# Moving the last segment's memory reads from the projections into the attention, on GpSimd's queue

## The chip, the cores and the metric

The kernel runs on one core of one Trainium2 chip. A core has TensorE (PE, matrix products; PEld is its weight loads), VectorE (DVE), ScalarE (ACT) and GpSimd (POOL), each with an instruction queue of its own that runs in order, and SyncE (SP), which issues most of the transfers. Transfers can also be issued from the queues of GpSimd and ScalarE. The metric is the device time of one execution in microseconds (us).

## The reference

Two attention layers on sequences of 2048 rows with 576 columns, 32 heads of 18, side by side in the output. A is softmax attention whose heads share one key and one value. B is cut into four segments of 512 rows and adds a memory that is filled segment by segment:

```python
phi = lambda t: jnp.where(t > 0, t + 1.0, jnp.exp(t))
for s in range(N):
    qs, ks, vs = q[:, :, s], k[:, :, s], v[:, :, s]
    logits = jnp.einsum("bhqd,bhkd->bhqk", qs, ks) * scale + mask
    p = _softmax(logits, axis=-1)
    a_dot = jnp.einsum("bhqk,bhkd->bhqd", p, vs)
    pq = phi(qs)
    num = jnp.einsum("bhld,bhde->bhle", pq, M)
    den = jnp.einsum("bhld,bhd->bhl", pq, z)[..., None] + 1e-6
    o = g * (num / den) + (1.0 - g) * a_dot
    outs.append(o)
    pk = phi(ks)
    M = M + jnp.einsum("bhld,bhle->bhde", pk, vs)
    z = z + jnp.einsum("bhld->bhd", pk)
```

To *ask the memory* is to compute `num` and `den` of a segment from its features `phi(q)`. The first segment's memory is empty, so three segments ask: s = 1, 2 and 3 (the last).

## The kernel before

**Stage 1, projections (to about 277 us).** A's chunks are projected, then B's segments s = 0 to 3. Every operand is a high and a low part, so one projection of 126 columns is 14 matmuls (L261). For each segment PE computes keys, values (14 matmuls for each quarter of rows and half of the heads, L513) and queries; ACT and DVE split the results in two parts and form features (L408, L414, L416); SP and ACT store them to DRAM. B's weights come in 15 parts on GpSimd's queue into buffers `wr`, two in each of two pools (L242), and are split by ACT (L251) and POOL (L252); the last three parts (12 to 14) are loaded within the key projections of s = 0, each after the split of an earlier part. For s = 3 the four last query projections are interleaved with this segment's asks: numerators `ask` (L444), evictions with the gate's factor (L451), denominators `total` (L592); beside them the bounds for the softmax (`bound`, L588), whose sum DVE reduces to `fm` (L613) and turns into a shift (L136).

**Stage 2, attention (277 to about 1365 us).** The order is written out by hand in 416 *turns* of three items. PE computes the scores E of an item (A: L945, B: L953), ACT its exponentials (L963); the second item of a turn is first copied by DVE from E to W (L960), and single halves are exponentials on DVE alone (L919 to L926, `BY_DVE`). Two turns later PE multiplies P with the values into O (L993). In B POOL clears the masked part of P in between (`affine_select`, L968). A block of A is 11 turns, a block of B two: A has turns 0 to 10, B 11 to 18, A 19 to 29, B 30 to 37, A 38 to 48, B 49 to 52, and so on. PE gets one piece of *fill* a turn: in turns 0 to 18 by the table `LATER` pieces of the four last values' sums that stage 1 left over (`late_value`, pairs of quarter and number of matmuls); from turn 20 (`ASK`) the asks of the segments in `LATE_ASK`, s = 1 and 2, as long as they last and only in turns of A; then the output projection (L796).

An ask in the attention (L852) comes in pieces of four matmuls, eight in the trace's records, for half of the columns; two pieces make one answer, which DVE writes over the features (L857). The features of a segment are loaded by `load_qf` from `qfB` into a tile `xh`, of which there are two, so that a third segment's features take the place of the first that were asked. The answers go from that tile to `numB` and `denB` by `store`, two turns after the ask. All these transfers are SP's. They are read back much later, when a segment's heads are weighed (`place` holds that back until enough segments are asked).

Of the kernel before, what the change touches and what calls it, by code (L numbers as in the profile page):

```python
# [8 lines left out]
F32 = mybir.dt.float32  # L9
# [13 lines left out]
C = 512  # L23
# [55 lines left out]
def attention_pair_kernel(ctx, tc, a_xT, a_w, a_wo, b_xT, b_w, b_wo, b_beta, ident_d, hmask_d, bmask_d, cmask_d, sel_d, zmask_d, selx_d, sely_d, out):  # L79
# [82 lines left out]
    with ExitStack() as ph:  # L162
# [256 lines left out]
        for s in range(NSEG):  # L419
# [19 lines left out]

            def ask(t, hold=lambda ins: ins):  # L440
                R = RT[t]
                pn = ps.tile([128, C], F32, name="mm", bufs=1)
                hold(
                    nc.tensor.matmul(  # L444
                        pn[:R], Mst[:R, t].rearrange("p h d -> p (h d)")[:, :R], fs[t][:R], start=True, stop=True
                    )
                )

                def answer():
                    nm = p2.tile([128, C], F32, name="nm", bufs=2)  # L450
                    hold(nc.scalar.activation(nm[:R], pn[:R], AF.Copy, scale=gt[:R, t : t + 1]))  # L451
                    nc.sync.dma_start(numB[s][126 * t : 126 * t + R], nm[:R])

                return answer


            for t in range(5):
# [18 lines left out]
                if not last or t == 4:  # L476
                    f = phi(pj[:126], 126, "kf" if t < 4 else "qf", 2 if t < 4 else 5, hold, e[0])
                    if t == 4:
                        fs[4] = f
# [23 lines left out]

            def value_sums(xh, xl, i, hf, pj, m0=0, m1=14):
                ops = []
                tk = slice(128 * i, 128 * i + 128)
                n = 288 if hf else 306
                for k in range(5):
                    hi, lo = (wv[:, k, 0], wv[:, k, 1]) if hf else (wBh[:, k, 1134:1440], wBl[:, k, 1134:1440])
                    ops += [(xh[:, k, tk], hi)] + ([(xl[:, k, tk], hi)] if k < 4 else []) + [(xh[:, k, tk], lo)]  # L510
                for m, (x, w) in enumerate(ops):
                    if m0 <= m < m1:
                        nc.tensor.matmul(pj[:, :n], x, w, start=m == 0, stop=m == len(ops) - 1)  # L513

            def values(i, hf):
                pj = ps.tile([128, C], F32, name="pj" if hf else "nd", bufs=4 if hf else 2)
                value_sums(xh, xl, i, hf, pj)
# [50 lines left out]
            for t in range(4) if not last else []:  # L568
# [8 lines left out]
                if s:  # L577
                    fs[t] = phi(pj[:126], 126, "qf", 5, e=e[0])
                    nc.sync.dma_start(qfB[s][:126, t], fs[t][:126])
# [9 lines left out]

            def total(pd, t):  # L590
                R, rows = RT[t], slice(32 * (t % 4), 32 * (t % 4) + 32)
                pin(nc.tensor.matmul(pd[rows], zst[:R, t], fs[t][:R], start=t < 4, stop=t > 0))  # L592

            for t in range(4) if last else []:
                pj = ps.tile([128, C], F32, name="pj", bufs=4)
                proj(pj[:126], wBh, wBl, xh, xl, 126 * t, 126, pin)
                answer = ask(t - 1 if t else 4, pin)
                if t < 2:
                    (fifth_bound if t else last_key)(pin)
                if t == 3:  # L600
                    pu, pd = (ps.tile([128, C], F32, name="nd", bufs=2) for _ in range(2))
                    for i in (0, 1, 2, 4):
                        total(pd, i)
                e = negative(pj[:126], 126, pin)
                magnitude(t, pj, pin)
                fs[t] = phi(pj[:126], 126, "qf", 5, pin, e)
                answer()
                if t == 3:
                    for i in range(5):
                        bound(pu, i, pin)  # L610
                    answer = ask(3, pin)
                    total(pd, 3)
                    pin(nc.vector.tensor_reduce(fm[:, 1 + s : 2 + s], pu, axis=AX.X, op=ALU.max))  # L613
                qp = split2(pt, pj[:126], 126, pin)
                store_parts(qp, 0, 126, qB[s], 7 * t, 7)
                if t == 3:
                    answer()
                    dn = p2.tile([128, C], F32, name="ph_e", bufs=2)
            if not last:
# [6 lines left out]
            if last:  # L626
                nc.vector.tensor_scalar(dn, pd, 1e-6, None, op0=ALU.add)
                nc.sync.dma_start(denB[s], dn)
                def late_value(i, m0, m1, pj, v, xh=xh, xl=xl, value_sums=value_sums):
# [197 lines left out]
    def load_qf(s):  # L827
        qfs[s] = px.tile([128, 5, C], F32, name="xh")
        nc.sync.dma_start(qfs[s][:126, :4], qfB[s][:126, :4])
        nc.sync.dma_start(qfs[s][: RT[4], 4], qfB[s][: RT[4], 4])  # L830

    def ask_memory():
# [5 lines left out]
        for s in LATE_ASK:  # L838
            qf = qfs[s]
            for t in (-1, 0, 1, 2, 3, 4):  # L840
# [22 lines left out]
                def store(k, s=s, t=t, qf=qf, dn=dn):  # L863
                    if t < 0:
                        nc.sync.dma_start(denB[s], dn)
                    elif t == 4:
                        nc.sync.dma_start(numB[s][126 * t :], qf[: RT[4], 4])
                        nc.sync.dma_start(denB[s][7:11], dn[103:107])
                        asked[0] = s
                    elif t == 3:  # L870
                        nc.sync.dma_start(numB[s][: 126 * 4].rearrange("(t r) c -> r t c", r=126), qf[:126, :4])

# [140 lines left out]
    def by_dve(c, hg):  # L1013

        return [x for n, x in enumerate(BY_DVE) if n < 2 or (c, hg) in third]

# [49 lines left out]
    def finish(k, ab, c, hg):  # L1066
# [64 lines left out]
    with tc.manual_schedule(engines={ENG.PE, ENG.Activation, ENG.DVE}):  # L1131
# [75 lines left out]

        for k in range(len(turns) + 2):
            now[0] = k
            exps = [scores(its[n], pr, i == 1) for i, (n, pr) in enumerate(turns[k])] if k < len(turns) else []  # L1210
            for i in (0, 2, 1) if len(exps) == 3 else range(len(exps)):
                exps[i]()
            if k in FLAG:
                loose_flag(k)
            if k < len(LATER) and LATER[k]:
                i, m = LATER[k]
                m0, pj = begun_value.pop(i) if i in begun_value else (0, psO.tile([128, C], F32, name="O" if i == 3 else "F"))
                if m0 + m < 14:
                    begun_value[i] = m0 + m, pj
                late_value(i, m0, m0 + m, pj, (pa.tile([128, D], F32, name="osb", bufs=2) if i > 1 else pa.tile([128, C], F32, name="oe", bufs=4))[:, :304] if m0 + m == 14 else None)  # L1220
            if k > len(turns):
                halve_heads(first, 0)
            if memory is None:
# [355 lines left out]
```

## Time and profile before

| | us |
|---|---|
| median of 3 runs (lowest to highest) | 1393.98 (1393.3 to 1396.08) |
| the profiled execution | 1394.57 |
| its span in the trace | 1392.9 |
| busy: ACT, DVE, POOL | 1205.8, 1032.6, 260.5 |

All times of rows in this document count from the start of the span of the profiled execution; granted clock 0.999. A row of the chain or of a timeline has the start, the duration and what ran, `x14` being fourteen instructions in one; a row of the waits has the waiting instruction, what it waited for, the sum of the time, how often and the longest. Matmul records overlap, since matmuls are pipelined: the distance between two starts is what one costs, not its record. Behind a transfer in the list of issues stand its KB and the median us from issue to landing.

### The profile page before, as it was taken

To read this page: it belongs to the slowest core of one execution; us is meant where nothing else is said; L and a number is where in the kernel's file an instruction comes from. 1 tells how busy PE (TensorE), PEld (TensorE's weight loads), DVE (VectorE), ACT (ScalarE), POOL (GpSimd) and SP (SyncE) were. 2 spreads that over 40 slices of the span, in tenths; PEclk is the share of its full clock that TensorE was granted. 3 is DMA by queue.
4 is the path that set the end of the run, shared out by engine and by line. 5 is a ranking of instruction groups with operands and counts; after the bars stand their busy time and mean duration, and the time that the engine had idled before them with its cause. 6 is when DMAs were issued, how large, how long until landed. Compare 5 with 4: busy or idle time off the path is not lost.

```text
span 1392.9 us, 41210 instructions
## 1 busy us (share of the span) xinstructions
PE 1379.1 (99%) x17455; PEld 835.6 (60%) x17455; DVE 1032.6 (74%) x1509; ACT 1205.8 (87%) x1497; POOL 260.5 (19%) x388
## 2 busy tenths in 40 slices
PE   9999999999999999999999999999999999999998
PEld 6778888755554555555555555555555555555558
DVE  6565463388787887777888877876878778887884
ACT  4543453599999999999999999999999999999992
POOL 2462120012313211312110022113010220001002
PEclk9999999999999999999999999999999999999999
DMA  9876556575564545332322442232103321120023
GB/s 285 261 230 185 180 198 204 188 208 181 153 182 158 147 145 162 101 113 77 105 67 71 141 152 63 85 120 79 52 35 100 104 76 42 31 71 21 18 64 132
DMA packets 88638, 173.67 MB, mean 125 GB/s; under 512 B 12308, under 2 KB 20109, under 8 KB 88018
## 3 DMA queue, kind: packets, MB, share of 16 engines
q1 hardware_dynamic: 81614, 158.91, 36.6%
q0 software_dynamic: 2368, 7.13, 1.8%
q10 hardware_dynamic: 4464, 4.92, 1.1%
q8 instruction: 139, 2.28, 0.7%
q14 instruction: 53, 0.43, 0.1%
HBM read 99.65 MB, written 70.67 MB: 122 GB/s over the span
## 4 chain that ended last, share of the span: by engine, by line
PE 88%; DVE 4%; ACT 3%; DMA 2%; issue 1%; POOL 1%; SPq 0%; DVEq 0%; POOLq 0%; ACTq 0%
PE O L993 33%; PE E L945 20%; PE F L796 11%; PE pj L261 11%; PE E L953 3%; ACT P L963 3%; PE nd L513 2%; DVE W L960 2%; PE pj L513 2%; PE E L1280 2%; PE pj L293 1%; PE F L852 1%; PE F L513 1%; DMA wr<-b_w 1%; DMA vseg<-vB 0%
## 5 line engine op out<-in xcount | busy, mean ns | idle before, releaser
L963 ACT ACTIVATE P<-E 128x1024 f32<-128x1024 f32 (+1 forms) x800 | 783.4, 1066 | 2.0 <-PE E L945 1.6
L960 DVE COPY W<-E 128x1024 f32<-128x1024 f32 (+2 forms) x416 | 453.1, 1089 | 142.2 <-PE E L945 84.1
L993 PE MATMUL O<-P,VA 128*32 128x256 f32 x7504 | 506.8, 379 | 0.0
L963 ACT ACTIVATE P<-W 128x1024 f32<-128x1024 f32 (+1 forms) x330 | 366.8, 1112 | 6.8 <-DVE W L960 6.3
L993 PEld LDWEIGHTS O<-P,VA 128*32 128x32 f32 x7504 | 258.8, 110 | 137.7 <-issue 4.7
L945 PE MATMUL E<-xl,kstA 56*128 56x512 f32 x1920 | 317.3, 430 | 2.1 <-ACT P L963 1.8
L945 PEld LDWEIGHTS E<-xl,kstA 56*128 56x128 f32 x1920 | 155.0, 184 | 159.1 <-issue 94.7
L968 POOL TENSOR_SCALAR_AFFINE_SELECT P<-P 128x256 f32<-128x256 f32 (+1 forms) x192 | 94.6, 493 | 393.4 <-ACT P L963 384.1
L780 POOL TENSOR_TENSOR xh<-xh,rb 126x512 f32<-126x512 f32 (+1 forms) x55 | 70.7, 1308 | 428.7 <-DVE PD L926 185.1
L796 PE MATMUL F<-woB,xh 126*32 126x192 f32 (+1 forms) x1920 | 126.6, 338 | 0.0
L993 PE MATMUL O<-PD,VA 128*32 128x256 f32 x688 | 88.9, 379 | 0.0
L796 PEld LDWEIGHTS F<-woB,xh 126*32 126x32 f32 (+1 forms) x1920 | 38.6, 108 | 74.8 <-issue 69.6
L993 PE MATMUL O<-P,vseg 128*32 128x256 f32 (+2 forms) x1536 | 81.4, 344 | 0.3
L127 DVE TENSOR_TENSOR qp<-pj,qp 126x512 fp32r<-126x512 f32 (+1 forms) x54 | 36.9, 686 | 54.4 <-ACT ph_e L408 32.8
L1002 DVE COPY oe<-O 128x512 f32<-128x512 f32 x64 | 44.2, 691 | 42.6 <-PE O L993 40.8
L261 PE MATMUL pj<-xh,wBh 128*126 128x512 f32 x180 | 72.5, 403 | 0.0
L919 DVE TENSOR_SCALAR PD<-E 128x512 uint32<-128x512 f32 x86 | 59.2, 688 | 16.5 <-PE E L945 14.9
L261 PE MATMUL pj<-xh,wBl 128*126 128x512 f32 x180 | 71.0, 394 | 0.0
L125 ACT CAST qp<-pj 126x512 fp32r<-126x512 f32 (+1 forms) x54 | 31.5, 584 | 42.6 <-PE pj L261 32.6
L993 PEld LDWEIGHTS O<-P,vseg 128*32 128x32 f32 x1536 | 49.1, 110 | 25.3 <-issue 1.8
L796 PE MATMUL F<-woA,xh 126*32 126x192 f32 (+1 forms) x960 | 63.9, 338 | 0.0
L924 DVE SCALAR_TENSOR_TENSOR PD<-PD,n 128x512 f32<-128x512 f32 x86 | 59.5, 692 | 3.0
(238 smaller groups left out, 1570.1 us busy)
## 6 DMA issues: line engine op xcount, KB each, us to landing
stB<-kB SPq DMA_DIRECT2D x96, 144.0 KB
stB<-qB SPq DMA_DIRECT2D x32, 288.0 KB
xl<-qA SPq DMA_DIRECT2D x30, 288.0 KB
oA<-oe SPq DMA_DIRECT2D x32, 256.0 KB
oB<-oe SPq DMA_DIRECT2D x32, 256.0 KB
qA<-qp SPq DMA_DIRECT2D x16, 504.0 KB
kB<-qp SPq DMA_DIRECT2D x16, 504.0 KB
qB<-qp SPq DMA_DIRECT2D x16, 504.0 KB
```

Of the source, the lines that this page charges most:

```text
L261: hold(nc.tensor.matmul(dst, w[:, c0 : c0 + M], x, start=i == 0, stop=i == len(ops) - 1))
L513: nc.tensor.matmul(pj[:, :n], x, w, start=m == 0, stop=m == len(ops) - 1)
L780: ins = tc.keep_in_program_order(nc.gpsimd.tensor_tensor(dst, a, b, op=op))
L796: nc.tensor.matmul(dst[32 * j : 32 * j + 32], parts[ab, c][: RT[t], t, r0 : r0 + 32], wo[ab][: RT[t], t, c0 : c0 + n], start=start, stop=stop,
L919: v.tensor_scalar(y, e, EXP_A, EXP_B, op0=ALU.mult, op1=ALU.add)
L924: lambda: stt(p, p, POLY[1], u, op0=ALU.add, op1=ALU.mult),
L945: nc.tensor.matmul(e[:, j], kstA[rows, 128 * kt : 128 * kt + 128], st[rows, h, :], start=True, stop=True)
L960: gate.append(nc.vector.tensor_copy(src[:, hs, :n], e[:, hs, :n]))
L963: nc.scalar.activation(p[:, hs, :n], src[:, hs, :n], AF.Exp, scale=SCALE)
L968: nc.gpsimd.affine_select(diag, diag, pattern=[[0, 2], [0, m], [1, 128]], base=0, channel_multiplier=-1, compare_op=ALU.is_ge, fill=0.0)
L993: nc.tensor.matmul(o[32 * j : 32 * j + 32, q0 : q0 + n], v, p[:, j % 2, p0 : p0 + n], start=m == hf == 0, stop=last and hf == 1,)
L1002: nc.vector.tensor_copy(osb, o)
```

## The change

The parts that belong together:

- Segment 3 is asked in the attention too. `ask`, `answer`, `total`, the evictions and the stores leave stage 1; its features go to `qfB[3]` instead. `ask_memory` now yields in every turn from 20 on, those of B too, so that 36 pieces take the turns 20 to 55, as 24 took before.
- The transfers of asks (`load_qf`, `store`) are issued from GpSimd's queue. The features of segment 3 are loaded at turn 32 or later, when the first asked segment is stored.
- The values' sum of quarter 2 (`values(2, 1)`) is back in stage 1; `LATER` has three others, done by turn 7.
- The weight parts 12 to 14 have buffers of their own and are loaded as soon as these exist.
- The first block has no half on DVE, and turn 0 no copy W; feature buffers go from five to three; `place` waits for one segment more.

```diff
-LATE_ASK, ASK = (1, 2), 20
-LATER = [(2, 14), (3, 14), (0, 3), None, (0, 3), (0, 4), None, (0, 4), None, None, (1, 3), None, (1, 3), None, (1, 2), (1, 2), (1, 2), None, (1, 2)]
+LATE_ASK, ASK = (1, 2, 3), 20
+LATER = [(3, 14), (0, 14), (1, 3), None, (1, 3), (1, 4), None, (1, 4)]
...
-            wrs[i] = (p1 if i % 2 and i < 10 else pt).tile([128, 648], F32, name="wr", bufs=2)[:, :n]
+            if i < 12:
+                wrs[i] = (p1 if i % 2 and i < 10 else pt).tile([128, 648], F32, name="wr", bufs=2)[:, :n]
+            else:
+                wrs[i] = p2.tile([128, 504], F32, name="wr2", bufs=3)
...
         p2 = ph.enter_context(tc.tile_pool(name="p2", bufs=1))
+        for i in (12, 13, 14):
+            load_wpart(i)
...
-                    if t < 3:
-                        load_wpart(12 + t)
-            if s and not last:
+            if s:
                 nc.sync.dma_start(qfB[s][: RT[4], 4], fs[4][: RT[4]])
...
                 proj(pj[:126], wBh, wBl, xh, xl, 126 * t, 126, pin)
-                answer = ask(t - 1 if t else 4, pin)
                 if t < 2:
                     (fifth_bound if t else last_key)(pin)
-                if t == 3:
-                    pu, pd = (ps.tile([128, C], F32, name="nd", bufs=2) for _ in range(2))
-                    for i in (0, 1, 2, 4):
-                        total(pd, i)
                 e = negative(pj[:126], 126, pin)
                 magnitude(t, pj, pin)
-                fs[t] = phi(pj[:126], 126, "qf", 5, pin, e)
-                answer()
+                qp = split2(pt, pj[:126], 126, pin)
+                store_parts(qp, 0, 126, qB[s], 7 * t, 7)
+                f = phi(pj[:126], 126, "qf", 3, pin, e)
+                nc.sync.dma_start(qfB[s][:126, t], f[:126])
                 if t == 3:
+                    values(2, 1, "mm", 1)
+                    pu = ps.tile([128, C], F32, name="nd", bufs=2)
                     for i in range(5):
                         bound(pu, i, pin)
-                    answer = ask(3, pin)
-                    total(pd, 3)
                     pin(nc.vector.tensor_reduce(fm[:, 1 + s : 2 + s], pu, axis=AX.X, op=ALU.max))
...
-        nc.sync.dma_start(qfs[s][:126, :4], qfB[s][:126, :4])
-        nc.sync.dma_start(qfs[s][: RT[4], 4], qfB[s][: RT[4], 4])
+        nc.gpsimd.dma_start(qfs[s][:126, :4], qfB[s][:126, :4])
+        nc.gpsimd.dma_start(qfs[s][: RT[4], 4], qfB[s][: RT[4], 4])
...
-                        nc.sync.dma_start(denB[s], dn)
+                        nc.gpsimd.dma_start(denB[s], dn)
...
-        return [x for n, x in enumerate(BY_DVE) if n < 2 or (c, hg) in third]
+        return [x for n, x in enumerate(BY_DVE) if (n or c or hg) and (n < 2 or (c, hg) in third)]
...
-            return (ab, c) in parts or len(parts) - filled[0] // FILL < 2 and asked[0] >= min(2, len(parts) + 1)
+            return (ab, c) in parts or len(parts) - filled[0] // FILL < 2 and asked[0] >= min(3, len(parts) + 2)
...
         at(ASK + 4, 0, lambda: True, lambda k: load_qf(2))
+        at(ASK + 12, 0, lambda: asked[0] >= 1, lambda k: load_qf(3))
...
-            elif k >= ASK and all(its[n][0] == "A" for n, pr in turns[k]) and next(memory, None) is None:
+            elif k >= ASK and next(memory, None) is None:
```

How the change moves instructions shows in the order of the engines' programs. POOL's rows at the start of B's first segment, before (`wr` are raw weight parts, `wBl` their low halves, `Mbd` the memory, `bands` the mask's bands):

```order
L242 DMA wr<-b_w 128x504
L395 MEMSET Mbd 128x285
L396 MEMSET mx 128x285
...
L402 MEMSET mz 128x790
L501 MEMSET vch 128x128
L252 TENSOR_TENSOR wBl<-wr,wBh 128x504
L242 DMA wr<-b_w 128x504
L252 TENSOR_TENSOR wBl<-wr,wBh 128x504
L242 DMA wr<-b_w 128x504
L252 TENSOR_TENSOR wBl<-wr,wBh 128x504
L242 DMA wr<-b_w 64x504 x2
```

And of the change:

```order
L245 DMA wr<-b_w 128x504
L245 DMA wr_856<-b_w 128x504
L245 DMA wr_858<-b_w 128x504
L245 DMA wr_860<-b_w 64x504 x2
L400 MEMSET Mbd 128x285
```

The last four transfers, for three parts, moved ahead of the clearing and of every split that stood between them.

PE's rows from the end of the last projection to the second score, before (`nd<-qf,mz` are totals, `mm<-qf,mz` an ask, `nd<-aq,kbB` bounds, `E<-st_126,kstA` scores):

```order
L261 MATMUL pj<-xh,wBl 126x512
L444 MATMUL mm<-qf,mz 126x512
L592 MATMUL nd<-qf,mz 32x512 x4
L588 LDWEIGHTS kbB
L588 MATMUL nd<-aq,kbB 32x512
...
L444 MATMUL mm<-qf,mz 126x512
L592 MATMUL nd<-qf,mz 32x512
L945 MATMUL E<-st_126,kstA 128x512 x6
```

Of the change (`mm<-woB,xh` are the values' matmuls, 14 in all):

```order
L264 MATMUL pj<-xh,wBl 126x512
L499 MATMUL mm<-woB,xh 128x288
L499 MATMUL mm<-woB,xl 128x288
...
L574 LDWEIGHTS kbB
L574 MATMUL nd<-aq,kbB 32x512
L918 MATMUL E<-st_127,kstA 128x512 x6
L499 MATMUL O<-woB,xh 128x288
```

Asks and totals are gone, and a values' sum stands ahead of the bounds; behind the first scores comes a late value in the bank O, where before it was F.

PE's rows in a turn of B from turn 30 on, before (scores `E<-stB`, products `O<-P,vseg`):

```order
L953 MATMUL E<-stB 128x512 x4
L953 MATMUL E<-stB 128x384 x2
L993 MATMUL O<-P,vseg 32x256 x8
L993 MATMUL O<-P,vseg 32x192 x4
L953 MATMUL E<-stB 128x384 x2
```

Of the change:

```order
L926 MATMUL E<-stB 128x512 x4
L926 MATMUL E<-stB 128x384 x2
L825 MATMUL F<-xh,woA 32x256 x4
L966 MATMUL O<-P,vseg 32x256 x8
L966 MATMUL O<-P,vseg 32x192 x4
L926 MATMUL E<-stB 128x384 x2
```

The four matmuls of a piece of an ask, which the trace records as eight, stand between the scores and the products of every B turn from 30 to 37 and from 49 to 52.

POOL's rows in the turns 30 to 33; before, these are masks alone (`P<-P`) at this place. Of the change:

```order
L838 DMA denB_111<-rb 128x512
L844 DMA numB_107<-xh 126x4x512
L941 AFFINE_SELECT P<-P 128x2x128 x4
L941 AFFINE_SELECT P<-P 128x4x128
L840 DMA numB_107<-xh 72x512
L941 AFFINE_SELECT P<-P 128x4x128
L841 DMA denB_111<-rb 4x512
L941 AFFINE_SELECT P<-P 128x2x128
L802 DMA xh<-qfB_116 126x2048
L941 AFFINE_SELECT P<-P 128x2x128 x3
L941 AFFINE_SELECT P<-P 128x4x128
L803 DMA xh<-qfB_116 72x512
```

The stores of segment 1's answers (1008 KB, then 144 KB, `numB`) and the load of segment 3's features into the same tile (`xh<-qfB`) now stand between the masks, in the queue that both share.

More of the change, by code (lines that the diff above doesn't have):

```diff
@@ L438, in magnitude @@
                 hold(nc.scalar.activation(aqs[t][:R], pj[:R], AF.Abs))
[L440 to L454, printed above, removed]
             for t in range(5):
@@ L512, in value_sums, with values @@
                     if m0 <= m < m1:
[L513 to L517, printed above, removed]
+                        hold(nc.tensor.matmul(pj[:, :n], x, w, start=m == 0, stop=m == len(ops) - 1))
+            def values(i, hf, nm=None, bufs=None):
+                pj = ps.tile([128, C], F32, name=nm or ("pj" if hf else "nd"), bufs=bufs or (4 if hf else 2))
+                value_sums(xh, xl, i, hf, pj, hold=pin if last else lambda ins: ins)
                 hs = slice(16 * hf, 16 * hf + 16)
@@ L577, in attention_pair_kernel @@
                 if s:
-                    fs[t] = phi(pj[:126], 126, "qf", 5, e=e[0])
+                    fs[t] = phi(pj[:126], 126, "qf", 3, e=e[0])
                     nc.sync.dma_start(qfB[s][:126, t], fs[t][:126])
@@ L588, in bound @@
                 hold(nc.tensor.matmul(pu[rows], kbB[:R, t], aqs[t][:R], start=t < 4, stop=t > 0))
-            def total(pd, t):
-                R, rows = RT[t], slice(32 * (t % 4), 32 * (t % 4) + 32)
-                pin(nc.tensor.matmul(pd[rows], zst[:R, t], fs[t][:R], start=t < 4, stop=t > 0))
             for t in range(4) if last else []:
@@ L864, in store @@
                     if t < 0:
-                        nc.sync.dma_start(denB[s], dn)
+                        nc.gpsimd.dma_start(denB[s], dn)
                     elif t == 4:
-                        nc.sync.dma_start(numB[s][126 * t :], qf[: RT[4], 4])
-                        nc.sync.dma_start(denB[s][7:11], dn[103:107])
+                        nc.gpsimd.dma_start(numB[s][126 * t :], qf[: RT[4], 4])
+                        nc.gpsimd.dma_start(denB[s][7:11], dn[103:107])
                         asked[0] = s
                     elif t == 3:
-                        nc.sync.dma_start(numB[s][: 126 * 4].rearrange("(t r) c -> r t c", r=126), qf[:126, :4])
+                        nc.gpsimd.dma_start(numB[s][: 126 * 4].rearrange("(t r) c -> r t c", r=126), qf[:126, :4])
                 at(now[0] + 2, 0, lambda: True, store)
@@ L1206, in halve_heads, with late_values @@
             mixed(x[:88, 1], hi[:88, 1], raws[key], some[:88, 1:2])
[L1208 to L1214, printed above, removed]
+        def late_values(k):
             if k < len(LATER) and LATER[k]:
@@ L1220, in attention_pair_kernel @@
                 late_value(i, m0, m0 + m, pj, (pa.tile([128, D], F32, name="osb", bufs=2) if i > 1 else pa.tile([128, C], F32, name="oe", bufs=4))[:, :304] if m0 + m == 14 else None)
+        for k in range(len(turns) + 2):
+            now[0] = k
+            if k == 0:
+                psE.tile([128, 2, 512], F32, name="E")
+            exps = []
+            for i, (n, pr) in enumerate(turns[k]) if k < len(turns) else []:
+                exps.append(scores(its[n], pr, i == 1 and k > 0))
+            for i in (0, 2, 1) if len(exps) == 3 and k else range(len(exps)):
+                exps[i]()
+            if k in FLAG:
+                loose_flag(k)
+            late_values(k)
             if k > len(turns):
```

10 lines of the change are left out of this document (2 added, 8 removed).

## Prediction, made before the changed kernel ran

> **What bounds the kernel now.** I read the page's totals first, then windows of 35 us at the places that the change touches, then the chain of work that ended last inside them.
>
> ```profile
> PE 1379.1 (99%) x17455; PEld 835.6 (60%) x17455; DVE 1032.6 (74%) x1509; ACT 1205.8 (87%) x1497; POOL 260.5 (19%) x388
> ```
>
> ```profile
> 245.00:280.00 35.00, 34.55 (x174) 24.91 (x174) 14.89 (x25) 18.72 (x38) 0.00 (x0) 1.00 0.58 187
> 350.00:385.00 35.00, 34.27 (x484) 18.63 (x476) 26.61 (x35) 34.53 (x43) 11.96 (x25) 1.00 0.54 157
> 630.00:665.00 35.00, 35.00 (x518) 19.29 (x514) 24.51 (x32) 35.00 (x41) 11.91 (x17) 1.00 0.22 67
> ```
>
> Each window row gives the length, then busy time of PE, PEld, DVE, ACT and POOL, the granted clock (1.00), the DMA share and GB/s. At the end of the projections (245 to 280) PE is full and ACT half idle: PE instructions taken out there shorten the run. In the attention both PE and ACT are full (35.00 of 35.00 at 630): PE work that is moved in there is hidden only as far as PE has a gap, and such gaps lie in the turns of B alone (34.27 at 350). The change moves work from the first kind of place into those gaps.
>
> **The change part by part.** All sums are against the profiled execution's own 1394.57 us.
>
> *A. Weight loads with their own buffers.* Waits and chain at s=0:
>
> ```profile
> ACT wBh L251 <- DMA wr<-b_w: 4.9, 2, 2.6
> PE tr L432 <- DVE qf L416: 1.6, 1, 1.6
> ```
>
> ```profile
> 87.45 7.32 DMA wr<-b_w
> ```
>
> A load issued late, behind a POOL split, lands after 7.32 us; ACT waits 4.9 us in two pieces for such loads, its later exponentials slip, and PE idles 1.6 us before the transposes (L432). In the changed order the four loads stand ahead of the clearing of Mbd, some ten microseconds sooner, so even 7.32 us end before ACT comes to them. PE is what sets the end here: **-1.6** (0 if the features are late for another reason; no more than the gap).
>
> *B. The end of the projections.* The chain from the first of the last four projections to the second score:
>
> ```profile
> 254.55 3.24 PE pj L261 x14
> 257.79 0.86 PE mm L444 x2
> ...
> 262.78 1.09 PE mm L444 x2
> ...
> 267.61 0.86 PE mm L444 x2
> ...
> 271.71 0.86 PE mm L444 x2
> 272.57 1.20 PE nd L592 x6
> ...
> 273.82 0.59 PE nd L592
> 274.41 0.43 PE nd L588 x2
> 274.84 1.05 PE mm L444 x2
> 275.90 0.98 PE nd L592 x2
> 276.87 0.90 PE E L945 x6
> 277.77 2.06 PE F L513 x14
> ```
>
> Asks (L444) go: 0.86 + 1.09 + 0.86 + 0.86 + 1.05 = 4.72. Totals (L592) go: 1.20 + 0.59 + 0.98 = 2.77. The values' sum that comes back costs 2.06, the price of the same 14 matmuls at 277.77. The five bounds (L588), most of which lay among the totals, now stand alone: five at half their pair's 0.43 are 1.1, against 0.43 on the chain, so +0.6. Together 7.49 - 2.06 - 0.6 = 4.8 us, and the first E starts at about 272.0 instead of 276.87. That the bounds wait for ACT's magnitudes is covered by the values' 2.06 us in front of them.
>
> What is late next is the bank of the first late value in turn 0, which the bounds' sum held and DVE must have read:
>
> ```profile
> 274.88 0.69 DVE L613 TENSOR_REDUCE fm<-nd 128x1 f32<-128x512 f32 x1 [0.81 <-PE nd L588]
> ...
> 276.09 0.68 DVE L136 TENSOR_SCALAR sht<-nd 128x512 f32<-128x512 f32 x1
> ```
>
> These two, 1.37 us behind the last bound, outlast the first E's 0.90 by 0.4 to 0.5. So **-4.4** (range -3.5 to -5). The removed evictions (ACT), stores (SP) and the totals' addition (DVE) lie beside PE and give nothing; the DVE half of the first block's exponentials goes too, and there PE with two values' sums is longer than three exponentials on ACT, so it costs nothing.
>
> *C. Turns 10 to 18 lose their pieces of late values.* A block of B is two turns; one with two such pieces:
>
> ```profile
> 314.31 0.78 PE E L953 x10
> 315.09 0.46 PE F L513 x2
> 315.56 1.11 PE O L993 x24
> 316.67 0.83 PE E L953 x6
> 317.50 0.46 PE F L513 x2
> 317.97 1.33 PE O L993 x24
> ```
>
> 317.97 + 1.33 - 314.31 = 4.99. A block without such pieces runs at ACT's pace, seen in POOL's masks, which follow ACT's exponentials:
>
> ```profile
> 357.25 0.42 POOL L968 TENSOR_SCALAR_AFFINE_SELECT P<-P 128x256 f32<-128x256 f32 x1 [28.96 <-ACT P L963]
> ...
> 360.30 1.42 POOL L968 TENSOR_SCALAR_AFFINE_SELECT P<-P 128x512 f32<-128x512 f32 x2 [0.22 <-ACT P L963]
> 361.94 0.42 POOL L968 TENSOR_SCALAR_AFFINE_SELECT P<-P 128x256 f32<-128x256 f32 x1 [0.23 <-ACT P L963]
> ```
>
> 361.94 - 357.25 = 4.69. One such block gains 0.30, and the lighter blocks and A's turn 10 about 0.2 together: **-0.5** (0 to -1).
>
> *D. Twelve asks in the B turns 30 to 37 and 49 to 52.* That is six blocks with two each. An ask before, in an A turn:
>
> ```profile
> 353.73 0.64 PE L852 MATMUL F<-xh,woA 126*32 126x256 f32 x8
> ...
> 354.19 0.39 PE L993 MATMUL O<-PD,VA 128*32 128x256 f32 x2
> ```
>
> Eight matmuls, 354.19 - 353.73 = 0.46 us to the next product, the same as a value piece. So each block becomes that of C: 0.78 + 1.11 + 0.83 + 1.33 = 4.05 plus 0.92 is 4.97, which is 0.28 over ACT's 4.69. Six blocks give 1.7; the lead that PE has from the A turns before them takes a little: **+1.5**. The bounds: 0, if all is hidden, and 12 x 0.46 = 5.5, if nothing is. DVE's evictions, one in two turns, stay beside the copies.
>
> *E. GpSimd's queue.* POOL works in order, and the load of the fourth segment's features into the second segment's tile has to wait until that tile's answers are stored: POOL stands at the load, and the masks behind it (rows of the order above), and PE's products behind those. In the clock of before, the mask of 357.25 is the block's first and the first half of 360.30 its fifth, so the 144 KB store behind it issues at about 361.0; that issue, one more and two masks later POOL reaches the load at about 363.3. The trace has no such store from POOL; the nearest rows:
>
> ```profile
> 326.48 0.56 POOL L636 DMA_DIRECT2D vB<-oe  x1 [0.44 <-POOL P L968]
> ```
>
> ```profile
> DMA to landing us min/median/max: 3.6/3.6/3.6
> ```
>
> ```profile
> DMA  5300000000000688887777775564358977679999
> ```
>
> ```profile
> kstA<-kA POOLq DMA_DIRECT2D x6, 144.0 KB, 5.1
> mzB<-mz POOLq DMA_DIRECT2D x2, 395.0 KB, 4.8
> wr<-b_w POOLq DMA_DIRECT2D x4, 324.0 KB, 6.9
> wr<-b_w POOLq DMA_DIRECT2D x4, 252.0 KB, 4.9
> ```
>
> ```profile
> 365.35 0.86 PE L993 MATMUL O<-P,vseg 128*32 128x256 f32 x12
> ```
>
> An issue takes 0.56. The second row is that same transfer's landing, 3.6 us (152 KB, in the attention). The third is the DMA engines' busy tenths in 40 slices of 350 to 385, 0.875 us each: idle from about 352 to 361, then 6 to 8. The last four are medians in the projections, where 144 KB took 5.1. With 3.6 the store lands at 364.6, the load has issued at 365.2, two masks of 0.42 end at 366.0, and the products of 365.35 start **0.65** late; with 5.1 they are 2.15 late; with 6.9, the longest of these rows, 3.95. Nothing gives it back, since ACT has no slack behind. I take **+1.3**, a landing of 4.25 between the first two: the place is the attention, but the store goes out just as other traffic starts. Ends: 0 and 4.
>
> The Trainium skill, page "DMA: Bandwidth & Descriptors", section "Anatomy of one DMA — SWDGE (gpsimd) path", gives about 2.0 us plus the bytes at 436 GB/s, an estimated 2.3 us for 144 KB, and by it this term would be 0. The measured 3.6 and 5.1 are above it and decide the sum; what a short landing does is the first rival.
>
> The Trainium skill, page "SBUF — State Buffer", in its trap "DVE blocks DMA", says that GpSimd can't write descriptors while DVE runs a two-port copy within SBUF; that speaks against moving transfers to this queue. No row here shows it: the issue at 326.48 took 0.56 like the rest.
>
> *F. The rest costs nothing.* The third segment's features now load at turn 7 beside the loads for B: 0, at most 1 if those come late. Three feature buffers instead of five: each is used again two projections (6.5 us) later, longer than any landing above. The mzB load is half as large again, and has until turn 20. From turn 56 on the order is that of before.
>
> The sum: -1.6 - 4.4 - 0.5 + 1.5 + 1.3 = -3.7, so 1390.9. The profiled execution stands 0.6 above the median of 1393.98; I go half of that down: **1390.5**.
>
> **The rivals.**
>
> *1. POOL's wait is covered.* The store lands within 2.95 us (365.35 - 0.84 - 0.56 - 361.0), and E is 0: 1390.5 - 1.3 = **1389.2**. For it: DMA is idle until the store goes out. Against: the shortest landing in the rows is 3.6.
>
> *2. The B turns take most of it back.* E comes at its upper end, 3.95, and A gives nothing since POOL's splits still follow ACT's: 1390.5 + 2.65 + 1.6 = **1394.8**; with one of the two, 1392 or 1393. For it: blocks full on both engines; against A failing: a 4.9 us wait with a named load.
>
> *3. Slower: the large store blocks POOL.* The same load also waits for the 1008 KB of answers, issued at about 355.9. From 252 to 324 KB the landing grew by 2.0 us; carried on, 1008 KB land after 4.9 + 756/72 x 2.0 = 26 us, at 382, and the products are 382 + 1.4 - 365.35 = 18 us late: 1390.5 - 1.3 + 18 = **1407**. It decides from a landing of about 8 us on (365.35 - 1.4 - 355.9). Against it: 395 KB took 4.8, less than 324, so the slope is hardly the size's, and DMA is idle when this store goes out.
>
> *4. The change doesn't shorten the projections' end,* since the first scores wait for ACT or DVE there: B is 0, 1390.5 + 4.4 = **1394.9**. Against: ACT is busy for 18.72 of 35 there.
>
> **How the numbers follow.** Forecast 0.48 (1388.5 to 1392), rival 1 0.15, rival 2 0.24, rival 3 0.08, rival 4 0.05. The range **1388.0 to 1394.9** leaves out rival 3, and the tails below and above. A measurement of this kernel tells about 0.2% (2.8 us) from no change: faster is below 1391.2, slower above 1396.8. Faster: seven tenths of the forecast and nearly all of rival 1, 0.34 + 0.14, and a little of rival 2, is 0.50; slower: rival 3 and a tail, 0.10; within: 0.40.
>
> **What would show it.** A: no wait of ACT for wr, and no PE gap before the transposes. B: the first E near 270.5 (4.8 and 1.6 earlier). D: B blocks 30 to 37 at 4.9 to 5.0 between equal masks. E: a POOL wait for a DMA at the feature load, a PE gap at products in turn 32 or 33; one of over 4 us makes the prediction wrong, and so does a first E that isn't 6 us sooner.

## The result, and the profile after

The changed kernel is **slower** by 0.7%: 1404.95 us median of 6 runs (1402.8 to 1408.65) against 1394.49 beside it (1393.05 to 1398.85), ratio 1.0073 with a 95% interval of 1.0052 to 1.0094. The forecast was 1390.5 with a range of 1388.0 to 1394.9. The profiled execution has a span of 1401.4 us.

Where the time went is seen first by laying the traces over each other. The scores are computed in the same order in both kernels, so the start of the same score matmul can be compared (us from the start of the span; no. 2562 is one of the output's matmuls behind the last score; "mended" is the kernel f5 of the experiments):

```
score matmul no.         0      6     66    120    228    354   2562
before               276.8  279.8  307.5  324.2  365.0  414.2  1357.5
changed              272.6  276.6  303.4  325.7  367.4  423.2  1366.2
mended (f5)          269.4  273.3  300.2  316.8  358.7  408.6  1351.8
```

The change is ahead by 4.2 us at the first score, not by the 6.4 of the prediction's steps A and B. It loses 5.6 between no. 66 and no. 120 (the first blocks of B), 0.9 up to no. 228, and 6.6 more up to no. 354. From there to the end the distance stays within 0.5 us. So three places hold the whole result, and at none of them did the prediction put a cost above 1 us.

Two windows of the kernel before, at places that the prediction doesn't show, then windows of the changed kernel, columns as before (length; busy PE, PEld, DVE, ACT, POOL; granted clock; DMA share; GB/s):

```profile
310.00:316.00 6.00, 5.96 (x82) 3.77 (x85) 3.71 (x4) 6.00 (x9) 3.38 (x7) 1.00 0.69 210
399.00:404.00 5.00, 4.98 (x74) 2.37 (x72) 4.93 (x8) 4.75 (x5) 0.00 (x0) 1.00 0.38 123
```

```profile
245.00:280.00 35.00, 31.41 (x185) 26.35 (x185) 14.56 (x24) 19.40 (x37) 0.64 (x5) 1.00 0.66 214
310.00:316.00 6.00, 2.70 (x39) 1.58 (x35) 1.65 (x2) 3.63 (x5) 2.88 (x6) 0.96 0.78 218
316.00:322.00 6.00, 5.67 (x47) 3.33 (x51) 1.83 (x2) 3.69 (x5) 1.32 (x4) 0.50 0.79 220
...
399.00:404.00 5.00, 0.84 (x6) 0.19 (x2) 2.20 (x4) 0.53 (x1) 0.00 (x0) 1.00 0.71 208
404.00:408.00 4.00, 3.92 (x36) 1.89 (x38) 3.87 (x8) 3.41 (x4) 0.58 (x1) 0.57 0.49 170
630.00:665.00 35.00, 35.00 (x524) 19.57 (x524) 25.79 (x34) 34.97 (x41) 10.50 (x13) 1.00 0.29 89
```

PE, all but full in these places before, now stands still three times: 3.6 us short in the first row, 3.3 in the second, 4.2 in the fourth. Behind two of the stalls PE is busy again but at a granted clock of 0.50 and 0.57: 24 products (`O`) that took 1.11 to 1.33 us before take 2.50 at 317.84. The half clock lasts some 7 and 3.5 us, and the second stall, of 3.0 us, costs 5.6 by the table. (The Trainium skill, "TensorE: Matmul & The Clock Gate", section "What's actually happening", has two clock states, full and half, decided by activity in a window of about 3.4 us that runs freely. The 0.50 agrees; the length of a gap alone does not decide it here, as will be seen.)

What ends the three waits, in the view of waits for PE, one fence for each stretch:

```profile
PE nd L499 <- ACT kn L508: 2.8, 1, 2.8
```

```profile
PE E L926 <- DMA stB<-ones_d: 3.5, 2, 3.0
```

```profile
PE E L918 <- DVE W L933: 4.2, 1, 4.2
```

All three lead to transfers that were late. **First (252).** ACT stood before a CAST into a `qp` buffer, which may be overwritten once its last contents have landed in DRAM. The row of that CAST, before, and of the changed kernel:

```profile
245.41 0.58 ACT L125 CAST qp<-pj 126x512 fp32r<-126x512 f32 x1 [4.63 <-DMA kB<-qp]
```

```profile
247.37 0.59 ACT L125 CAST qp<-pj 126x512 fp32r<-126x512 f32 x1 [7.74 <-PE nd L499]
```

7.74 us instead of 4.63. The profile names PE in the second, since a PE event came last by its account; but ACT needs nothing of that product, and in the repeats below the same wait, 7.75 us long, is put down to the landing. SyncE's rows of the changed kernel show that the stores of keys (`kB<-qp`) were issued late, and GpSimd's rows what had been issued before them:

```profile
233.46 5.74 SPq L156 DMA_DIRECT2D st<-shA  x2
240.96 2.47 SPq L131 DMA_DIRECT2D kB<-qp  x3
```

```profile
225.72 0.57 POOL L802 DMA_DIRECT2D xh<-qfB  x1 [25.69 <-DMA qfB<-qf]
226.28 0.54 POOL L803 DMA_DIRECT2D xh<-qfB  x1
```

SyncE needed 5.74 us for two small loads (1.27 before). Its own waits say why, before and in the changed kernel:

```profile
SPq L156 <- DMA qB<-qp: 0.7, 1, 0.7
```

```profile
SPq L156 <- DMA qB<-qp: 4.4, 1, 4.4
```

Between the two loads it stood until a store of queries had landed, 11.1 us after its issue at 227.85 (before: 7.2 us). In flight beside that store was the load of segment 1's features, 1152 KB, in two parts. Its large part left at about the same time as on SyncE's queue (225.72, against 227.61 before); its 144 KB part left some 20 us sooner, and SyncE, without this load, sent a load of A's queries (`xl<-qA`, 288 KB) already at 225.61 and not near 249.

**Second (316).** The chain through the wait:

```profile
310.57 5.63 DMA stB<-ones_d
316.19 0.14 issue
316.33 1.51 PE E L926 x4
317.84 2.50 PE O L966 x24
```

```profile
295.07 0.55 POOL L802 DMA_DIRECT2D xh<-qfB  x1 [13.91 <-PE F L499]
```

The last load of B's second stack was issued at 310.57; before, at 308.63, while PE was 4 us later. At 295.07 GpSimd had issued 1008 KB of segment 2's features, at 296.59 the rest; before, SyncE issued them at 334.31, behind those loads. Again SyncE stood for landings of its own loads. Its longest such waits among the loads of this stack's keys and ones, before and in the changed kernel:

```profile
SPq L707 <- DMA stB<-qB: 1.7, 2, 1.3
```

```profile
SPq L681 <- DMA stB<-qB: 2.7, 1, 2.7
```

For the loads of this stack's keys and ones these waits came to 8.7 us in all, against 2.1 before.

**Third (403).** DVE waits, in its own order, at the reciprocal of B's first sums, with the copies W behind it that ACT and PE need:

```profile
DVE sm L718 <- DMA sm<-oB: 4.2, 1, 4.2
```

```profile
387.55 0.87 POOL L844 DMA_DIRECT2D numB<-xh  x1 [5.46 <-DVE xh L830]
```

The sums go to DRAM with O and come back. The row above is the 1008 KB store of segment 2's answers, issued beside that round trip; before, it went out at 424. But the round trip also began late. DVE's copy of O and SyncE's store of it, before and in the changed kernel:

```profile
380.03 0.69 DVE L1002 COPY oe<-O 128x512 f32<-128x512 f32 x1
380.75 0.37 SPq L1008 DMA_DIRECT2D oB<-oe  x1
```

```profile
381.98 0.68 DVE L975 COPY oe<-O 128x512 f32<-128x512 f32 x1
385.75 0.37 SPq L981 DMA_DIRECT2D oB<-oe  x1
```

Before, the store left 0.03 us after the copy; now SyncE, which works in order, was still busy with loads and left it lying for 3.1 us. From its issue to the reciprocal the sums then took 16.1 us (before at most 13.5, as DVE didn't wait). DVE came to the reciprocal 14.9 us after the copy: 3.1 + 16.1 - 14.9 makes the wait, a late start and a longer trip. SyncE's delay began at the stack's loads: at 373.37 it had stood 2.6 us for a landing (0.2 before), while the load of segment 3's features, issued by GpSimd at 365.06 and 367.34, was coming in until 373.0.

Three theories were put to the test: **C**, crowded transfers (large ones make those land late that PE waits for, with the half clock behind); **Q**, GpSimd's in-order queue between the masks; **P**, the asks in B's turns not being hidden.

### The profile page after: what moved, and what is told of

Read it like the earlier page. It is cut to its first block, busy times and chain, and to the rows that moved or that the text cites. A ratio compares the mean times of both kernels' runs of the same rounds, so it can differ in the third digit from the quotient of the medians.

```text
span 1401.4 us, 41387 instructions
## 1 busy us (share of the span) xinstructions
PE 1379.7 (98%) x17531; PEld 839.6 (60%) x17531; DVE 1033.9 (74%) x1506; ACT 1204.0 (86%) x1493; POOL 269.0 (19%) x405
## 4 chain that ended last, share of the span: by engine, by line
PE 72%; DVE 4%; DMA 3%; ACT 2%; issue 1%; SPq 1%; POOL 0%; DVEq 0%; ACTq 0%
PE O L966 33%; PE E L918 19%; PE F L769 11%; PE E L926 4%; PE E L1262 2%; ACT P L936 2%; DVE W L933 2%; DMA stB<-shB 1%; PE F L825 1%; PE pj L264 1%; DMA oB<-oe 1%; DMA stB<-qB 0%; DVE sm L718 0%; DMA stB<-ones_d 0%; DMA stB<-kB 0%
## 5 line engine op out<-in xcount | busy, mean ns | idle before, releaser
L926 PE MATMUL E<-stB 56*128 56x256 f32 (+3 forms) x512 | 60.3, 348 | 4.1 <-DMA stB<-ones_d 3.5
```

The lines of the kernel that those rows point to most:

```text
L926: nc.tensor.matmul(e[:, j, c0 : c0 + 512 - 128 * k], st[rows, 4 + h, ks], st[rows, h, 128 * k :], start=True, stop=True)
```

## The experiments

All eleven ran with the same kernel before beside them; its medians were 1394.3 to 1394.5.

**e1: segment 2's features later.** The load stays on GpSimd's queue, but behind a copy W of turn 26.

```diff
+            if s == 2:
+                tc.keep_in_program_order(ins)
+                tc.add_manual_dep(ins.ins, gate[-1].ins.name, AFTER, reason="not before this turn")
...
-        at(ASK + 4, 0, lambda: True, lambda k: load_qf(2))
+        at(ASK + 6, 0, lambda: True, lambda k: load_qf(2))
```

> Only the load of segment 2's features (1152 KB on GpSimd's queue) is held back from turn 7 to turn 26, where the transfer engines are idle. Theory C (crowded transfers): in the changed kernel this load, issued at 295, delays the loads of B's second stack, so PE waits 3.0 us at 316 and then runs at a granted clock of 0.50 for some 6 us; without it the wait goes, the clock stays at 1.00 there, and the time is 1404.95 - 5 = about 1400. Rival Q (GpSimd's in-order queue, the masks behind the feature load of segment 3): nothing changes, 1405. Rival P (the asks in turns of B are not hidden): nothing changes, 1405.

1398.48, ratio 1.0022 (1.0009 to 1.0035): 6.5 less than the changed kernel. The wait at 316 is gone, the clock there is 1.00, and scores no. 66 and 120 are 2.5 and 2.7 us ahead of before, so nothing is lost there. The other two waits stayed, and the third was longer:

```profile
DVE sm L718 <- DMA sm<-oB: 5.8, 1, 5.8
...
PE E L921 <- DVE W L936: 5.7, 1, 5.7
```

SyncE left O's store lying for 4.0 us here, and the sums took 16.7 from its issue. Theories Q and P, which had 1405, fall as main causes.

**e2: everything on SyncE's queue.** `nc.gpsimd.dma_start` to `nc.sync.dma_start` in `load_qf` and `store`.

> All transfers of the asks go back to SyncE's queue; the asks stay in the turns of B. Theory C: on SyncE's queue the order of issue itself keeps the feature load behind the stacks and the large store behind the sums' loads, so both PE waits (316 and 403) go and the time is about 1391 to 1394. Rival Q: the masks are free too, but its price was at most 4 us: 1401 or more, with the waits at 316 and 403 still there. Rival P: 1405, or worse.

1394.88, ratio 0.9999 (0.9983 to 1.0014), 10 less than the changed kernel. The waits at 252 and 316 are gone; the first score starts at 269.3. The third wait is left, 2.7 us long (the clock stayed at 1.00 behind it), and not because of a slow round trip: the sums took 11.1 us from the issue of O's store, less than before had room for. The store itself was late, 6.5 us behind DVE's copy, since SyncE had stood for the landing of segment 3's features, now on its own queue:

```profile
SPq L680 <- DMA xh<-qfB: 4.7, 1, 4.7
```

The asks in B's turns are all in this kernel.

**e4: segment 2's answers later too.** e1, and the three stores of segment 2's answers six turns later in the kernel's text.

```diff
-                at(now[0] + 2, 0, lambda: True, store)
+                at(now[0] + (8 if s == 2 and t >= 3 else 2), 0, lambda: True, store)
```

> As the kernel with the late feature load, and the stores of segment 2's answers (1152 KB) six turns later as well. Theory C: the wait of DVE for the sums (4.2 us at 402) comes from that store's traffic beside the store of O and the sums' load; both waits go, about 1394 or less. Rival S (SyncE is late there for another reason: its stack loads): the wait at 403 stays, as in the kernel with the late feature load alone, about 1400. Rivals Q and P: 1405.

1407.74, ratio 1.0086 (1.0059 to 1.0114): a miss, and the most instructive one. The edit did not do what it was made for. The 1008 KB store still left right behind its answer, as in e1 (383.62, with PE 6.0 us sooner there), beside the sums' loads:

```profile
389.59 0.87 POOL L852 DMA_DIRECT2D numB<-xh  x1 [5.48 <-DVE xh L833]
```

All the same the third wait is gone: the sums took at most 11.4 us here. So that store alone does not make the wait, and e4 does not tell what does. Two losses came in instead. The edit moved other rows on GpSimd: segment 1's last store and the load of segment 3's features now stood directly ahead of the masks of a whole block. The waits of POOL and of PE there, and windows:

```profile
POOL xh L803 <- issue: 4.5, 1, 4.5
```

```profile
PE O L974 <- POOL P L949: 2.4, 1, 2.4
```

```profile
373.00:377.00 4.00, 3.95 (x32) 2.04 (x34) 0.00 (x0) 0.07 (x1) 3.48 (x8) 0.57 1.00 205
```

POOL stood 4.5 us at the load, PE 2.4 for the masks, and then ran at 0.57: score no. 246, which was 0.2 us behind before's at no. 240, is 4.9 behind. That is theory Q's mechanism, real but in another place than in the changed kernel. The second loss, 7 us between no. 2544 and no. 2562, is at the end: from 1340 on PE still has 256 matmuls of the output projection, against 128 in the changed kernel. The likely reason, not tried: a segment is weighed only when the kernel's text has stored its answers, so the projection starts later and its pieces run out of turns.

**e5: asks only in A's turns again.** The condition on `its[n][0] == "A"` is put back.

> The asks stay out of the turns of B again, as before the change, and so run to a later turn; transfers as in the changed kernel. Theory C: the wait at 316 stays with its half clock; the store of segment 2's answers moves to another place, so the wait at 403 goes or moves: 1398 to 1404. Rival P: the asks in B turns are the price; 1395 or less. Rival Q: the load of segment 3's features no longer stands between masks; a gain of 1 to 4 us, 1401 to 1404.

1413.27, ratio 1.0123 (1.0095 to 1.015), worse than every theory had it. The wait at 316 stayed. The asks run on past turn 55 and the output projection starts later; at the end (1340 to 1402) PE still has 288 of its matmuls, against 128 in the changed kernel:

```profile
L769 PE MATMUL F<-woB,xh 126*32 126x192 f32 (+1 forms) x288 | 14.8, 330 | 1.4 <-DVE osb L793 1.4
```

The trace puts 8.5 us there (no. 2562 is 19.7 behind before's, after 11.2 at no. 552); PE also waits 2.5 and 1.6 us for stack loads near 460. So the asks belong in B's turns if all three segments ask in the attention. As a test of theory P this run is impure, since it also puts the output projection off; P falls by e1, e2 and f5, which keep those asks in B's turns and take 6.5, 10 and 16 us less than the changed kernel.

**f1: segment 1's features on SyncE's queue, nothing else.**

```diff
-        nc.gpsimd.dma_start(qfs[s][:126, :4], qfB[s][:126, :4])
+        (nc.sync if s == 1 else nc.gpsimd).dma_start(qfs[s][:126, :4], qfB[s][:126, :4])
```

(and so for the second part).

> Only the load of segment 1's features goes back to SyncE's queue; the rest is the changed kernel. Theory C: on GpSimd's queue this load (issued at 225.7) puts SyncE's stores of the last segment's keys back, ACT waits for the landing of one of them and PE idles 2.8 us at 252; on SyncE's queue it goes out in two parts around them, PE's wait goes and the first score starts some 3 us sooner (269 to 270 instead of 272.6); the later waits stay: about 1402. Rival W (the wait at 252 comes from the earlier pace or another order of the projections, whatever the queue): the wait stays, 1405.

1400.62, ratio 1.0043 (1.0029 to 1.0058). The CAST's wait is 4.62 us, as before the change, PE's wait is gone, and the first score starts at 269.1:

```profile
243.63 0.59 ACT L125 CAST qp<-pj 126x512 fp32r<-126x512 f32 x1 [4.62 <-DMA kB<-qp]
```

In e1, where the load is still on GpSimd's queue, the row reads:

```profile
247.39 0.59 ACT L125 CAST qp<-pj 126x512 fp32r<-126x512 f32 x1 [7.75 <-DMA kB<-qp]
```

The first wait is settled: 3.5 us at the first score, by the queue of one load. (In e1, e4, e5 and f6, where the load is on GpSimd's queue too, PE's wait was 3.3 to 4.8 us with the half clock behind it, and the first score 1.5 to 2.9 us later than in the changed kernel: this place varies.)

**g1: the same edit in the old kernel.** Only the feature loads of segments 1 and 2 on GpSimd's queue, in the kernel before the change.

> The kernel before with one edit: the two feature loads (1152 KB each) on GpSimd's queue, nothing else of the change. Theory C: the first load alone, issued near 226 beside SyncE's stores, brings PE's wait of 2.8 us near 254 into the old kernel, and the second, which GpSimd's queue now issues some 15 us earlier, beside the loads of B's stacks, may bring another: 1397 to 1400. Rival W (those waits belong to the new order of work): 1394.5, no wait.

1397.88, ratio 1.0028 (1.0019 to 1.0038): the queue of these two loads costs 3.6 us without any of the rest. The CAST waits 5.64 us instead of 4.63, PE waits twice (1.6 us at 236, 0.6 at 252), and the first score is 2.2 us late in this execution of 1396.32:

```profile
247.76 0.59 ACT L125 CAST qp<-pj 126x512 fp32r<-126x512 f32 x1 [5.64 <-DMA kB<-qp]
```

The second load, issued at 328 here, brought no wait.

**f6: DVE's reciprocals three turns later, in the changed kernel.**

```diff
-        d0, d1, d2, d3 = ... (2, 5, 3, 5) if (ab, c) == ("B", 0) else ...
+        d0, d1, d2, d3 = ... (2, 8, 3, 5) if (ab, c) == ("B", 0) else ...
```

> The changed kernel with one edit: DVE's reciprocals of B's first sums three turns later. Theory C: PE's gap of 4.15 us at 403 and the half clock behind it go, some 6 us: about 1399; the waits at 252 and 316 stay. Rival D (the asks make those turns long): 1405.

1400.79, ratio 1.0049 (1.0032 to 1.0066), 4.2 less, not the 6 expected; in this execution the wait at 252 was longer (3.8, with the half clock behind it). The third wait is gone, and its half clock. **f2**, the same edit in e2:

> All transfers on SyncE's queue as in the kernel e2, and DVE's reciprocals of B's first sums three turns later in its program. Theory C: what is left of the loss near turn 45 is DVE standing in order at the reciprocal for a late load of the sums, with W copies behind it; with three turns (8 us) more no wait is left, PE's gap of 2.7 us at 393 goes, 2 to 3 us less than e2, about 1392. Rival D (PE waits there because the asks make the turns too long): the gap or the loss stays, 1394.9.

1390.77, ratio 0.9977 (0.9963 to 0.9991), 4.1 less than e2. No wait of PE above 1 us is left between 240 and 420. Its runs lie in two groups (1389.5 to 1391.2, and 1393.6 to 1396.1); the profiled one of 1393.63 has a wait of PE of 2.2 us at 62, with the half clock behind it, in the first projections, which the edit doesn't touch.

**f5: the changed kernel with three mends.** Segment 1's features on SyncE as in f1, segment 2's held back as in e1, reciprocals three turns later. Stores and segment 3's load stay between the masks.

> The changed kernel with three mends: segment 1's features on SyncE, segment 2's features held back to turn 26 on GpSimd's queue, the reciprocals three turns later; the stores and segment 3's load stay between the masks on GpSimd's queue. Theory C: all three waits (252, 316, 403) go and the time is that of f2, 1391 to 1393. Rival Q (GpSimd's in-order queue costs too): 1 to 4 us more than f2.

**1388.9** (five runs, 1388.55 to 1389.49), ratio 0.9961 (0.9947 to 0.9975): 16 us less than the changed kernel and 5.6 less than before, the fastest of all. Its windows at the places of the three stalls:

```profile
245.00:280.00 35.00, 34.20 (x218) 27.59 (x216) 15.67 (x26) 21.89 (x40) 1.36 (x6) 1.00 0.72 223
...
316.00:322.00 6.00, 5.71 (x78) 3.04 (x70) 3.80 (x7) 6.00 (x10) 2.95 (x6) 1.00 0.50 152
...
399.00:404.00 5.00, 4.79 (x72) 2.72 (x64) 3.36 (x5) 5.00 (x7) 2.19 (x5) 1.00 0.31 87
```

Clock 1.00 and PE full throughout, ACT full in the attention. And POOL at the load of segment 3's features, with the store ahead of it:

```profile
353.54 0.54 POOL L843 DMA_DIRECT2D numB<-xh  x1
...
356.34 0.53 POOL L803 DMA_DIRECT2D xh<-qfB  x1 [0.72 <-issue]
```

The store landed after 2.3 us; POOL waited 0.7, and PE did not wait for a mask. The changed kernel's own trace has the same: its store, issued at 362.27, and POOL's wait at the load behind it:

```profile
DMA to landing us min/median/max: 2.3/2.3/2.3
```

```profile
POOL xh L802 <- issue: 0.7, 1, 0.7
```

Theory Q has no price in the order of the changed kernel.

**f3 and g2: the old weight loads**, in e2 and in f5, to size term A.

> e2 with the old loads of the weight parts 12 to 14. By the prediction's term A, 1.6 us more than e2, with the wait of ACT for the weights and PE's gap before the transposes back: 1396.5. If the own buffers do nothing: 1394.9.

> The mended kernel f5 (1388.9) with the old loads of the weight parts 12 to 14, to size term A in a kernel whose times lie within 1 us. Term A as predicted: 1390.5, with PE's gap before the transposes. If that gap was one execution's: 1388.9 to 1389.3.

f3: 1395.78, 0.9 more than e2, between the two expectations; but its first score is at 269.4, as in e2, and what it lost lies at the third wait (3.6 us, with the half clock behind it). g2: 1389.69 (1388.65 to 1391.68), 0.8 more than f5; PE waits 0.7 and 0.6 us before the transposes, and the first score is 1.4 late. So the own buffers are worth 1.4 us in one pair of traces, 0.1 in the other and about 0.8 by the medians, which with runs this wide is not far from nothing.

## Why the prediction was wrong

**The step that failed** is F, "the rest costs nothing", with its sentence on the third segment's features (s = 2, called segment 2 here): "0, at most 1 if those come late". The load at turn 7 cost 5.6 us in the traces (e1: 6.5 by the medians). The same step said nothing of segment 1's features, whose load moved too: 3.5 us at the first score in f1, 2.2 in g1. And no step asked what the sums' round trip would meet near turn 45: 6 us (f6: 4.2 by the medians). The part on GpSimd priced these transfers by what waits *in* that queue; their price was what they do to the queue they had left: SyncE's own loads and stores landed late beside them, and SyncE, in order, stood for those landings (4.4 us instead of 0.7 at the first place, 8.7 instead of 2.1 at the second) and issued late what PE needed. For segment 2 the order on SyncE had kept the load 39 us back, behind the loads of the stack. The Trainium skill, "DMA: Bandwidth & Descriptors", section "Queues, rings and completion order", says that each transfer engine takes turns between the queues that have work. The late landings fit that, but no run here shows the turns themselves; the prediction had no such step.

A first score that is not 6 us sooner was one of the prediction's own signs of being wrong; it was 4.2 sooner.

**The second omission** is the clock. A stall was priced by its own length; the runs show 0.50 to 0.57 behind those at 316 and 403, so 3.0 us cost 5.6.

Point by point, with f5 as the kernel that has the rest undisturbed. By how many us the same score starts sooner than before (turns 10 to 18 are no. 60 to 130, turns 30 to 37 no. 196 to 260, turns 49 to 52 no. 326 to 358):

```
score matmul no.      0     6    60   130   196   260   326   358  2562
f5                  7.4   6.4   6.7   7.7   7.4   5.9   6.4   5.7   5.7
e2                  7.5   6.5   6.8   7.8   7.4   5.9   2.7   1.9   2.0
```

- **A** (-1.6): about -0.8 by the medians of g2 and f5, and nothing at the first score in f3. The waits are those named, but with the old loads they came to 1.3 us in g2 and to none above 0.5 in f3: the 1.6 was one execution's.
- **B** (-4.4, first score 4.8 earlier): in f5 the first score is 7.4 us ahead of before and the second 6.4; less A's 1.4 (f5 against g2) 6.0 and 5.0, where 4.8 and 4.4 were said: right, and somewhat more. That the first late value waits for DVE's shift came true, 0.8 us instead of 0.4 to 0.5.
- **C** (-0.5): in turns 10 to 18 f5 gains 1.0, the upper end.
- **D** (+1.5) and **E** (+1.3): in turns 30 to 37 f5 gives 1.5 back, in turns 49 to 52 another 0.7, together 2.2. e2, which has no transfer of the asks on GpSimd's queue, gives back the same 1.5 in turns 30 to 37, and POOL's wait of 0.7 us doesn't reach PE: so this is D's, and E is 0. The first rival was right in that, with a landing of 2.3 us, under its 2.95.
- **Sum**: without F's omissions the prediction's terms, with E at 0 as in that rival, gave 1389.2; f5 measured 1388.9. The work moved as forecast, and the transfers undid it; but that the sum fits so closely is partly luck, since B and C came out larger than said, A smaller and D dearer.
- The **rivals**: the third came out near the time (1407), but by chance. Its mechanism, masks behind a wait in GpSimd's queue, did not act in the changed kernel; e4 shows that it can. No rival was a transfer that goes faster to its issue and crowds out another.

What stays open: what makes the sums late at 403. f6 and f5 show the price of DVE's wait, not what lengthens the way of the sums: segment 3's features (which held SyncE up in e2), segment 2's answers (which stood beside the sums in e4 too, without a wait) and the weights `woB` behind them were not separated. At the first place the load's queue, its early second part and the early load of A's queries came together in one edit. And how a transfer on one queue makes another's land late was read from landings and waits, not tried.

## What to carry to other kernels

A transfer that is moved to an idle queue is not only relieved of its order, it loses the protection that the order gave to the others: list for each one moved where it would be issued now, what the queue it left will issue sooner, and which awaited transfers are in flight there. A wait of an engine that works in order (here a reciprocal on DVE, with copies behind it) should stand far enough behind its transfer's usual round trip that a crowded one still fits. And in a kernel whose PE is full, price a stall of 3 us at 5 to 6.

## What the runs showed of the hardware

- **The half clock follows a gap of some 3 us, and below 3 not always.** It came with PE waits of 2.2 us (f2, at 62), 2.4 (e4, at 373), 2.6 (e5, at 317), 2.8 (f1, at 312) and with all nine of 3.0 to 5.7; not with 2.5 (f1, at 398), 2.7 (e2, at 393) and 2.8 (changed kernel, at 252). Each time, the ends of the runs left out, it lasted 3.4 or 6.8 us, also where PE was busy again: in the changed kernel from 315.53 to 322.36 and from 404.28 to 407.69.
- **144 KB from GpSimd to DRAM landed in 2.3 us** in the changed kernel (from 362.27) and in f5 (from 353.54), and took 5.1 in e4 (from 365.92) at a DMA share of 0.78.
- **With one load of 1152 KB on a second queue the first queue's small loads took 4 us more** (5.74 us for two, 1.27 before), as SyncE waited between them for a store to land that took 11.1 us and not 7.2. Beside it 288 KB more than before were in flight on SyncE's own queue.
